# The constant of every fourth unit, added by GpSimd instead of shifted in by TensorE

## The chip, the core and the metric

The kernel runs on one core of one Trainium2 chip. The metric is the device time of one execution in microseconds. The engines are named as the profile names them: PE (TensorE, with PEld for its weight loads), DVE (VectorE), ACT (ScalarE), GpSimd (POOL in the rows) and SP, which only starts transfers here.

## The reference

An attention over 32 inducing points, twice (first the points attend to the rows of x, then each row of x to the 32 results), and then, on its output, a layer with a rational activation:

```python
h = mab(I, x)                  # 32 inducing points attend to 12480 rows, 4 batches
x = mab(x, h)                  # each of the 49920 rows attends to the 32 results
h = x @ w_in                   # 128 -> 2048
P = a[0] + a[1] * h + a[2] * h**2 + a[3] * h**3
Q = 1.0 + np.abs(b[0]) * np.abs(h) + np.abs(b[1]) * h**2
out = (P / (Q + 1e-06)) @ w_out    # 2048 -> 128
```

## The kernel before

**Units.** A block is 480 rows of x; there are 26 of them in each of 4 batches. The 2048 columns of h are worked in 8 *units* of 2 x 128 columns, q = 0 to 7 of a block: 832 units in all, each a tile of 128 x 960. Two neighbouring units, 2k and 2k + 1, are a *pair* and share one tile u of 128 x 1920.

**What a unit goes through.** `first` makes h (scaled) on PE, two f16 matmuls into a PSUM tile hp; there are 3 such tiles. From h comes the magnitude, u = |h|. Then l = (u + k1) * (h + k2) is made, on DVE. On ACT, u becomes a logarithm and then a sigmoid, over whole pairs in place. Behind that, l = (l + k3) * u is made. `second` multiplies l by w_out on PE into the PSUM tile po, two f32 matmuls (four rows of the trace) in a unit.

**Even and odd units.** Where k2 enters h differs:

- An odd unit's h comes with k2 from its weights, and ACT takes the magnitude with k2 taken off again (the rows ACTIVATE u<-hp,all).
- An even unit's h comes without k2. DVE takes the magnitude by masking the sign bit (TENSOR_SCALAR u<-hp), and after that `moved` adds k2 to h in PSUM by two f16 matmuls of constants, 96 x 128 by 96 x 480: the *shift* (rows MATMUL hp<-same,by with LDWEIGHTS by). The DVE product l<-u,all,hp of that unit comes after the shift.

**Ticks.** `fast_ticks` writes the order of everything by hand; the instructions keep it on every engine. Tick t starts unit t:

- PE: the second half of unit t - 15, `first` of unit t + 1 between its two matmuls, and at an even t the shift of unit t.
- DVE: at an even t the mask of unit t; at an odd t the product l<-l,all,u of unit t - 13, which is even; at every t the product l<-u,all,hp of unit t - 1.
- GpSimd: at an odd t the product of the odd unit t - 12, `last_on_pool`, in two instructions: an add u<-l,all into the u of unit t - 13 and a product l<-u. The add writes where DVE's product of the same tick reads, and so waits for it.
- ACT: the magnitude at an odd t, and one logarithm or sigmoid of a pair in every tick, four and four in turn, with a table load at each change.

`side` then gives out the work of the attention and of the next batch (the tiles pd, a, asm, hl, pc, e and others) in portions, by a budget for DVE, GpSimd and PE that grows with each tick. `fetch` copies a finished po to oT on DVE, once in a block, in the tick of unit 7, before the product of unit t - 13. A GpSimd instruction of `side` stands in the same queue as the others. `general_ticks` is for other values of a and b and is not run here.

All operations go through one recording helper, so every row of the profile has its line, 177; the rows are told apart by their tiles.

Of the kernel before, what the change touches and what calls it, by code (L numbers as in the profile page):

```python
# [16 lines left out]
ALU = mybir.AluOpType  # L17
# [175 lines left out]
class Kernel:  # L193
# [350 lines left out]
    def plain(self, t):  # L544
        return t if self.fast else t.bitcast(F32)
# [343 lines left out]
    def fast_ticks(self, units):  # L889

        V, A, p = self.nc.vector, self.nc.scalar, self.params
        n = len(units)
        at = lambda t: units[t] if 0 <= t < n else None
        plain = lambda u: not self.shifted(u.key[2])

        def mask(u):
            V.tensor_scalar(out=u.u.bitcast(I32), in0=u.h.bitcast(I32), scalar1=0x7FFFFFFF, scalar2=None, op0=ALU.bitwise_and)  # L900

        self.first(units[0])
        for t in range(n + BEHIND + 3):
            u, last, d, done = at(t), at(t - 1), at(t - BEHIND), at(t - BEHIND - 2)
            group, turn = divmod(t - TURNS - 2, 2 * TURNS)
            w = at(2 * TURNS * group + 2 * (turn % TURNS))
            late = done and done.key[2] == 0
            if done and not late:
                self.second(done, (0,))
            if at(t + 1):  # L910
                self.first(at(t + 1))
            if done and not late:
                self.second(done, (1,))
            if u:
                if t % 2 == 0:
                    u.pair = self.mp.tile([P, 2, 2, BT], F32, tag="u", name=f"u{u.i}", bufs=self.rooms["u"])
                    u.u = u.pair[:, 0]
                    mask(u)
                else:
                    u.u = last.pair[:, 1]  # L920
                    if not plain(u):
                        A.activation(u.u, u.h, AF.Abs, bias=p.z_back, scale=1.0)
            if late:
                self.fetched = self.fetch()
            if t % 2 and d:
                V.scalar_tensor_tensor(out=d.g, in0=d.g, scalar=p.z_k3, in1=d.u, op0=ALU.add, op1=ALU.mult)
                self.last_on_pool(at(t - BEHIND + 1), d)
            if u and t % 2 and plain(u):
                mask(u)
            if last:  # L930
                last.g = self.new(last, "l")
                V.scalar_tensor_tensor(out=last.g, in0=last.u, scalar=p.z_k1, in1=last.h, op0=ALU.add, op1=ALU.mult)
            if u and plain(u):
                self.moved(u)
            self.run_act(turn == TURNS)
            if w and turn < TURNS:
                A.activation(w.pair, w.pair, AF.Ln, bias=LAM, scale=LAM / Z)
            elif w:
                A.activation(w.pair, w.pair, AF.Sigmoid, bias=p.lnc, scale=-2.0)
            self.side(u or units[-1])  # L940
            if late:
                self.second(done)
        self.fetch()
# [170 lines left out]
```

## Time and profile before

| | |
|---|---|
| median of 3 runs | 2430.82 us (2430.80 to 2431.76) |
| the profiled execution's own time | 2437.1 us |
| its span, first to last instruction | 2435.3 us |
| busy in the span: PE | 2241.4 us (92%) |
| ACT | 2235.6 us (92%) |
| DVE | 2160.0 us (89%) |
| GpSimd | 1450.1 us (60%) |
| mean granted clock of TensorE | 0.964 |

The busy time is a union: instructions of one engine overlap a little at their ends. An engine is idle where its next instruction waits; the rows name what ended the wait. The first 150 us are start-up, with the first batch's attention and the conversion of the weights, and hold few units.

### The profile page before, as it was taken

Reading aid. Unit: us, or ns where it says so; the run is one execution under the profiler, and the core shown is the slowest. Engines: PE = TensorE matmul, PEld = TensorE weight load, DVE = VectorE, ACT = ScalarE, POOL = GpSimd, SP = SyncE. Lnnn points to the kernel's source line nnn. Section 1 sums busy time; section 2 is a strip of 40 time slices with the busy share of each in tenths; the row PEclk is TensorE's granted clock in tenths of the full one; section 3 lists DMA queues with packets and bytes.
Section 4 is the critical chain, followed back from the end, with each engine's and each line's share of the span. In section 5 each row is a group of like instructions: output and inputs, shape, how many; then the busy total and the mean of one; then the engine's idle time right before and its main releaser. Section 6 shows DMA issues by size and latency. Waiting matters only on the chain.

```text
span 2435.3 us, 25780 instructions
## 1 busy us (share of the span) xinstructions
PE 2241.4 (92%) x8462; PEld 1079.8 (44%) x8462; DVE 2160.0 (89%) x2386; ACT 2235.6 (92%) x1590; POOL 1450.1 (60%) x997
## 2 busy tenths in 40 slices
PE   4379999899999999999999899999999999999997
PEld 2244544344545444444445444444444444444443
DVE  1679999889999988999999889989999999999995
ACT  1069999999989999999899999999999999999996
POOL 0315666566656666666566666756666666666666
PEclk7569999999999999999999999999999999999999
DMA  9312210032022211310222130001101000000000
GB/s 236 85 33 85 81 50 17 13 85 65 25 65 82 77 42 42 79 50 29 85 82 59 31 90 29 17 13 53 49 21 41 29 17 28 17 18 20 13 16 18
DMA packets 117113, 121.03 MB, mean 50 GB/s; under 512 B 13289, under 2 KB 115561, under 8 KB 116969
## 3 DMA queue, kind: packets, MB, share of 16 engines
q1 hardware_dynamic: 116969, 119.28, 17.5%
q8 instruction: 69, 1.13, 0.2%
q14 instruction: 75, 0.61, 0.1%
HBM read 80.89 MB, written 25.56 MB: 44 GB/s over the span
## 4 chain that ended last, share of the span: by engine, by line
PE 37%; ACT 31%; DVE 16%; issue 10%; SPq 2%; DMA 2%; POOL 1%; DVEq 0%; POOLq 0%; ACTq 0%
ACT u L177 25%; PE po L177 22%; PE hp L177 9%; DVE l L177 8%; ACT L177 5%; DVE u L177 3%; PE pd L177 3%; SPq L177 2%; DMA xTw<-x_c 1%; DVE cv L177 1%; DVE asm L177 1%; PE pgt L177 1%; PE pl L177 1%; DMA at<-hl 1%; POOL l L177 1%
## 5 line engine op out<-in xcount | busy, mean ns | idle before, releaser
L177 PE MATMUL po<-l,w_out 128*128 128x480 f32 x3328 | 1572.9, 577 | 6.5 <-POOL l L177 4.9
L177 DVE SCALAR_TENSOR_TENSOR l<-u,all,hp 128x960 f32<-128x960 f32 x832 | 1003.8, 1207 | 110.6 <-ACT u L177 95.8
L177 POOL TENSOR_TENSOR l<-u 128x960 f32<-128x960 f32 x416 | 930.9, 2238 | 34.6
L177 POOL TENSOR_SCALAR u<-l,all 128x960 f32<-128x960 f32 x416 | 445.4, 1071 | 824.1 <-DVE l L177 714.6
L177 PEld LDWEIGHTS po<-l,w_out 128*128 128x128 f32 x3328 | 619.0, 192 | 385.8 <-issue 220.0
L177 ACT ACTIVATE u<-u,all 128x1920 f32<-128x1920 f32 x416 | 775.4, 1888 | 1.2
L177 ACT ACTIVATE u<-u 128x1920 f32<-128x1920 f32 x416 | 738.0, 1798 | 9.9 <-DVE l L177 8.7
L177 PE MATMUL hp<-at,st 128*128 128x480 f16 x1664 | 480.8, 371 | 60.1 <-DVE l L177 52.7
L177 DVE SCALAR_TENSOR_TENSOR l<-l,all,u 128x960 f32<-128x960 f32 x416 | 529.5, 1273 | 4.8 <-ACT u L177 4.8
L177 DVE TENSOR_SCALAR u<-hp 128x960 int32<-128x960 int32 x416 | 477.2, 1147 | 27.8 <-PE hp L177 26.1
L177 ACT ACTIVATE u<-hp,all 128x960 f32<-128x960 f32 x416 | 435.1, 1046 | 50.5 <-PE hp L177 46.4
L177 PEld LDWEIGHTS <-st 128*128 128x128 f16 (+1 forms) x1872 | 182.5, 98 | 554.6 <-issue 538.5
L177 ACT ACT_TABLE_LOAD x234 | 300.2, 1283 | 4.7 <-PEq L1107 0.7
L177 PE MATMUL hp<-same,by 96*128 96x480 f16 x832 | 239.3, 368 | 48.1 <-DVE u L177 41.7
L177 PEld LDWEIGHTS <-by 96*128 96x128 f16 x832 | 82.0, 99 | 239.1 <-issue 211.7
L177 DVE COPY oT<-po 128x480 f32<-128x480 f32 x104 | 67.9, 653 | 52.8 <-PE po L177 52.5
L177 PEld LDWEIGHTS pd<-HT,xTb 128*120 128x120 f32 x832 | 101.6, 195 | 15.8 <-issue 12.2
L177 PE MATMUL pd<-HT,xTb 128*120 128x32 f32 x832 | 97.9, 273 | 1.5 <-DMA xTb<-x_c 1.5
L177 PE MATMUL po<-at,st 128*128 128x480 f16 x208 | 59.1, 366 | 0.0
L177 ACT ACTIVATE a<-a 120x512 f32<-120x512 f32 (+2 forms) x21 | 14.9, 727 | 42.0 <-DVE a L177 41.9
L177 ACT ACTIVATE e<-e,nmc 128x960 f32<-128x960 f32 (+1 forms) x16 | 15.6, 993 | 32.9 <-DVE nmc L177 32.8
L177 PE MATMUL pa<-ident,a 120*128 120x120 f32 (+1 forms) x112 | 17.4, 281 | 28.8 <-DVE a L177 25.0
(110 smaller groups left out, 610.4 us busy)
## 6 DMA issues: line engine op xcount, KB each, us to landing
xTb<-x_c SPq DMA_DIRECT2D x104, 240.0 KB, 2.8
out<-oT SPq DMA_DIRECT2D x104, 240.0 KB, 2.0
xTa<-x_c SPq DMA_DIRECT2D x78, 240.0 KB, 3.5
x<-x_t SPq DMA_DIRECT2D x78, 240.0 KB, 4.5
at<-hl SPq DMA_DIRECT2D x416, 30.0 KB, 1.8
xw<-x_t SPq DMA_DIRECT2D x8, 720.0 KB, 14.2
xTw<-x_c SPq DMA_DIRECT2D x5, 960.0 KB, 12.6
raw<-w_in SPq DMA_DIRECT2D x4, 480.0 KB, 11.2
```

Of the source, the lines that this page charges most:

```text
L177: ins = call(*args, **kw)
```

## The change

In units 2 and 6 of a block (q % 4 == 2, every other even unit) the shift on PE is left out, so that their h stays without k2. Right after the mask of unit t, in tick t, GpSimd makes u + k1 into a new tile l, one instruction of 128 x 960. In tick t + 1 DVE's product of the unit is (h + k2) * l, where it was (u + k1) * h. Units 0 and 4 keep the shift, the odd units are as before.

```diff
-        V, A, p = self.nc.vector, self.nc.scalar, self.params
+        V, A, G, p = self.nc.vector, self.nc.scalar, self.nc.gpsimd, self.params
         n = len(units)
         at = lambda t: units[t] if 0 <= t < n else None
         plain = lambda u: not self.shifted(u.key[2])
+        added = lambda u: u.key[2] % 4 == 2
@@
             if u and t % 2 and plain(u):
                 mask(u)
-            if last:
+            if last and added(last):
+                V.scalar_tensor_tensor(out=last.g, in0=last.h, scalar=p.z_k2, in1=last.g, op0=ALU.add, op1=ALU.mult)
+            elif last:
                 last.g = self.new(last, "l")
                 V.scalar_tensor_tensor(out=last.g, in0=last.u, scalar=p.z_k1, in1=last.h, op0=ALU.add, op1=ALU.mult)
-            if u and plain(u):
+            if u and added(u):
+                u.g = self.new(u, "l")
+                G.tensor_scalar(out=u.g, in0=u.u, scalar1=1.0, scalar2=p.z_k1, op0=ALU.mult, op1=ALU.add)
+            elif u and plain(u):
                 self.moved(u)
```

GpSimd's queue, in the first batch. The names are tile, block, q and a running number, so l_7_6 is the l of block 7, unit 6. First before, then with the change:

```order
L177 TENSOR_SCALAR u_6_0_1552<-l_6_1_1580,all 128x960
L177 TENSOR_TENSOR l_6_1_1580<-u_6_0_1552 128x960
L177 TENSOR_SCALAR u_6_2_1578<-l_6_3_1629,all 128x960
L177 TENSOR_TENSOR l_6_3_1629<-u_6_2_1578 128x960
L177 TENSOR_SCALAR u_6_4_1627<-l_6_5_1670,all 128x960
```

```order
L177 TENSOR_SCALAR u_6_0_1540<-l_6_1_1568,all 128x960
L177 TENSOR_TENSOR l_6_1_1568<-u_6_0_1540 128x960
L177 TENSOR_SCALAR l_7_6_1790<-u_7_6_1786,all 128x960
L177 TENSOR_SCALAR u_6_2_1566<-l_6_3_1616,all 128x960
L177 TENSOR_TENSOR l_6_3_1616<-u_6_2_1566 128x960
```

The new add of unit 6 of block 7 stands behind the add and product for units 0 and 1 of block 6, and ahead of those for units 2 and 3.

DVE's queue around the same unit, before and with the change:

```order
L177 TENSOR_SCALAR u_7_6_1801<-hp_7_6_1772 128x960
L177 SCALAR_TENSOR_TENSOR l_7_5_1803<-u_7_4_1763,all,hp_7_5_1759 128x960
L177 COPY oT_5_1808<-po_5_0_1689 128x480
L177 SCALAR_TENSOR_TENSOR l_6_2_1610<-l_6_2_1610,all,u_6_2_1578 128x960
L177 SCALAR_TENSOR_TENSOR l_7_6_1827<-u_7_6_1801,all,hp_7_6_1772 128x960
```

```order
L177 TENSOR_SCALAR u_7_6_1786<-hp_7_6_1757 128x960
L177 SCALAR_TENSOR_TENSOR l_7_5_1788<-u_7_4_1748,all,hp_7_5_1744 128x960
L177 COPY oT_5_1793<-po_5_0_1675 128x480
L177 SCALAR_TENSOR_TENSOR l_6_2_1570<-l_6_2_1570,all,u_6_2_1566 128x960
L177 SCALAR_TENSOR_TENSOR l_7_6_1790<-hp_7_6_1757,all,l_7_6_1790 128x960
```

The order stays; the last of the five reads the tile l that GpSimd writes in place of u.

PE's queue behind the matmuls of po at that place, before and with the change:

```order
L177 LDWEIGHTS by
L177 MATMUL hp_7_6_1772<-same,by 128x480
L177 LDWEIGHTS by
L177 MATMUL hp_7_6_1772<-same,by 128x480
L177 LDWEIGHTS st_618
L177 MATMUL hp_8_0_1820<-at_2_0_1515,st_618 128x480
```

```order
L177 LDWEIGHTS st_618
L177 MATMUL po_5_0_1675<-at_1_0_1104,st_618 128x480
L177 LDWEIGHTS st_618
L177 MATMUL hp_8_0_1805<-at_2_0_1504,st_618 128x480
```

The two shift matmuls and their weight loads are gone, and the first product of the next unit follows at once.

## Rows read from the trace of the kernel before

**Rows 1.** The page: each engine's busy time in us, its share of the span, and its instructions.

```profile
span 2435.3 us, 25780 instructions
PE 2241.4 (92%) x8462; PEld 1079.8 (44%) x8462; DVE 2160.0 (89%) x2386; ACT 2235.6 (92%) x1590; POOL 1450.1 (60%) x997
```

**Rows 2.** The table of stages: the stretch, its length, and each engine's busy time in it.

```profile
150.00:700.00 550.00, 520.23 (x2048) 258.92 (x2048) 497.88 (x530) 524.98 (x373) 329.16 (x230) 0.96 0.19 55
700.00:1200.00 500.00, 480.27 (x1906) 233.81 (x1908) 465.30 (x502) 481.90 (x344) 310.44 (x218) 0.99 0.20 57
1200.00:1700.00 500.00, 481.30 (x1870) 231.09 (x1863) 464.59 (x495) 489.06 (x349) 317.77 (x220) 1.00 0.18 50
1700.00:2100.00 400.00, 382.65 (x1298) 182.92 (x1297) 376.19 (x356) 398.81 (x279) 255.40 (x158) 0.99 0.09 29
2100.00:2400.00 300.00, 282.54 (x851) 124.37 (x850) 273.58 (x253) 299.16 (x206) 192.69 (x118) 1.00 0.05 18
sum 2250.00, PE 2146.99 PEld 1031.10 DVE 2077.54 ACT 2193.90 POOL 1405.45; mean PE 429.40 PEld 206.22 DVE 415.51 ACT 438.78 POOL 281.09
```

The columns behind the length are PE, PEld, DVE, ACT and POOL busy, then the granted clock of TensorE, the share of the DMA engines and GB/s.

**Rows 3.** The list of waits between 150 and 2400 us: who waited for whom, us in total, times, the longest.

```profile
DVE l L177 <- ACT u L177: 95.8, 97, 3.4
PE hp L177 <- DVE l L177: 51.2, 84, 4.6
DVE oT L177 <- PE po L177: 40.1, 35, 2.4
PE hp L177 <- DVE u L177: 39.1, 34, 2.7
ACT u L177 <- PE hp L177: 35.3, 32, 4.8
DVE u L177 <- PE hp L177: 18.1, 19, 3.5
DVE l L177 <- PE hp L177: 11.8, 14, 2.9
ACT u L177 <- DVE l L177: 8.7, 14, 3.0
```

**Rows 4.** DVE in order of time, two pairs of units late in the run: start, duration in us, and in brackets the idle time before and what ended it. The mask at 2340.48 is that of a unit 2, the product l<-u,all,hp at 2343.93 the same unit's.

```profile
2338.23 1.21 DVE L177 SCALAR_TENSOR_TENSOR l<-l,all,u 128x960 f32<-128x960 f32 x1
2339.36 1.21 DVE L177 SCALAR_TENSOR_TENSOR l<-u,all,hp 128x960 f32<-128x960 f32 x1
2340.48 1.15 DVE L177 TENSOR_SCALAR u<-hp 128x960 int32<-128x960 int32 x1
2341.55 1.21 DVE L177 SCALAR_TENSOR_TENSOR l<-u,all,hp 128x960 f32<-128x960 f32 x1
2342.67 1.34 DVE L177 SCALAR_TENSOR_TENSOR l<-l,all,u 128x960 f32<-128x960 f32 x1
2343.93 1.20 DVE L177 SCALAR_TENSOR_TENSOR l<-u,all,hp 128x960 f32<-128x960 f32 x1
2345.06 1.15 DVE L177 TENSOR_SCALAR u<-hp 128x960 int32<-128x960 int32 x1
2347.28 1.21 DVE L177 SCALAR_TENSOR_TENSOR l<-u,all,hp 128x960 f32<-128x960 f32 x1 [1.08 <-ACT u L177]
```

**Rows 5.** GpSimd in order of time in the same stretch.

```profile
2339.61 1.07 POOL L177 TENSOR_SCALAR u<-l,all 128x960 f32<-128x960 f32 x1 [1.92 <-DVE l L177]
2340.76 2.23 POOL L177 TENSOR_TENSOR l<-u 128x960 f32<-128x960 f32 x1
```

**Rows 6.** ACT in order of time in the same stretch: the magnitude of one odd unit.

```profile
2346.20 1.04 ACT L177 ACTIVATE u<-hp,all 128x960 f32<-128x960 f32 x1
```

**Rows 7.** The page's groups of instructions: count, busy us, mean ns of one, and the idle time before them with what ended most of it.

```profile
L177 DVE SCALAR_TENSOR_TENSOR l<-u,all,hp 128x960 f32<-128x960 f32 x832 | 1003.8, 1207 | 110.6 <-ACT u L177 95.8
L177 POOL TENSOR_SCALAR u<-l,all 128x960 f32<-128x960 f32 x416 | 445.4, 1071 | 824.1 <-DVE l L177 714.6
L177 DVE SCALAR_TENSOR_TENSOR l<-l,all,u 128x960 f32<-128x960 f32 x416 | 529.5, 1273 | 4.8 <-ACT u L177 4.8
L177 PE MATMUL hp<-same,by 96*128 96x480 f16 x832 | 239.3, 368 | 48.1 <-DVE u L177 41.7
```

**Rows 8.** GpSimd and DVE in order of time at two places where the two meet, around 1224 and around 2401 us.

```profile
1224.08 1.05 POOL L177 TENSOR_TENSOR a<-a,asm 120x512 f32<-120x512 f32 x1
1224.36 1.78 DVE L177 SCALAR_TENSOR_TENSOR l<-l,all,u 128x960 f32<-128x960 f32 x1
...
2401.00 1.21 DVE L177 SCALAR_TENSOR_TENSOR l<-l,all,u 128x960 f32<-128x960 f32 x1
2401.26 1.89 POOL L177 TENSOR_SCALAR u<-l,all 128x960 f32<-128x960 f32 x1 [1.92 <-DVE l L177]
```

**Rows 9.** DVE in order of time: the two products that bound the first, and the two that bound the last, of the 205 intervals with a changed unit between 150 and 2400 us; in the last, the copy between them.

```profile
158.74 1.22 DVE L177 SCALAR_TENSOR_TENSOR l<-l,all,u 128x960 f32<-128x960 f32 x1
168.12 1.21 DVE L177 SCALAR_TENSOR_TENSOR l<-l,all,u 128x960 f32<-128x960 f32 x1
...
2389.51 1.21 DVE L177 SCALAR_TENSOR_TENSOR l<-l,all,u 128x960 f32<-128x960 f32 x1
2394.02 0.65 DVE L177 COPY oT<-po 128x480 f32<-128x480 f32 x1
2394.59 1.21 DVE L177 SCALAR_TENSOR_TENSOR l<-l,all,u 128x960 f32<-128x960 f32 x1
```

**Rows 10.** PE in order of time in the stretch of rows 4: the first product of the odd unit whose magnitude stands in rows 6.

```profile
2340.62 0.57 PE L177 MATMUL hp<-at,st 128*128 128x480 f16 x2
```

## The prediction

> **What bounds the kernel now.** The page is read first. Its engine shares name no single bound: PE 92%, ACT 92% and DVE 89% of a span of 2435.3 us [rows 1]. A start-up stage of some 150 us with little of the main loop blurs them, so the table of stages is read next [rows 2]. Between 150 and 2400 us, 2250 us in all, ACT is busy for 2193.9, PE for 2147.0, DVE for 2077.5 and GpSimd for 1405.5 us. ACT is the bound: it stands at 99.7% from 1700 us on, and is 25.0, 18.1 and 10.9 us short of the three stages before. In those stages PE is close behind it (520 of 550, 480 and 481 of 500 us).
>
> The list of waits tells why ACT falls short [rows 3]. ACT waits 35.3 us for a first product, 8.7 for DVE. PE waits 51.2 us for DVE to leave a PSUM buffer, and 39.1 us with the shift in hand, for the magnitude that has to be taken first. DVE waits 95.8 us for ACT and 40.1 + 18.1 + 11.8 = 70.0 us for PE; all its idle time in the five stages is 2250 - 2077.5 = 172.5 us. So two engines (ACT, PE) are tight, DVE has 7.7% to spare, GpSimd 38%.
>
> Last the order in time, for two pairs of units late in the run [rows 4 to 6]. I call the DVE product of a stored l and a stored u the *late product* (the rows l<-l,all,u); one stands in each pair. Look at what GpSimd does behind it: the late product ends at 2339.44, GpSimd's add starts at 2339.61, its product ends at 2340.76 + 2.23 = 2342.99. DVE comes to the next late product at 2342.67, and that one takes 1.34 us instead of 1.21: it ends 1.02 us after GpSimd's product.
>
> **What the change takes away.** 416 of the 832 shift matmuls, with their weight loads. They are 239.3 us of PE's time [rows 7], so 119.7 us go, 0.575 us in each changed unit. In the five stages 205 changed units lie, whose 118 us take PE from 2147 to 2029 us. Half of PE's 39.1 us of waiting for the magnitude goes too.
>
> **What it adds.** In each of the 208 changed units GpSimd makes one add of 128x960. The trace has this form: 1071 ns [rows 7]. 208 x 1.071 = 223 us bring GpSimd to 1673 us, 69% of the span: throughput is no question. DVE's instructions stay the same in number; the product of a changed unit reads one PSUM and one SBUF operand as before (1207 ns), with their places exchanged. I price that at nothing; no row has the exchanged form, the nearest are 1207 ns and, with both operands in SBUF, 1.21 us [rows 4], so both ends lie together. ACT's list does not change.
>
> **Where the add stands.** GpSimd's queue holds it behind the add and product of the tick before, and DVE's late product of the next tick meets it. From [rows 4, 5]: 0.17 us after a late product's end GpSimd begins 1.07 us of add, 0.08 later 2.23 us of product: done at +3.55. The new add can start at about +3.6 and ends at +4.68. DVE, without other work, is at its next late product at 2342.67 - 2339.44 = +3.2.
>
> These two operations do not run at once. [rows 8] show it both ways. GpSimd's 120x512 product runs from 1224.08 to 1225.13; a late product begun at 1224.36 ends at 1226.14, 1.01 later, and took 1.78 us. And a GpSimd add begun at 2401.26, while a late product ran to 2402.21, took 1.89 us: done 0.94 us after it. So there are two cases. If GpSimd's add is first, the late product ends at 4.68 + 1.01 = 5.7 us after the one before. If the late product is first (it waits already while GpSimd's product runs), it ends at 4.57 as now, but the add is done only at about 5.5, and the product of the changed unit, the next in DVE's queue, waits for that instead: from 4.49 to 5.56. Both cost about 1.1 us against the shortest interval of 4.57 (2339.44 to 2344.01). Behind the waiting DVE instruction stand the next magnitude and the next unit's product, and PE waits for the PSUM buffer that these leave.
>
> The Trainium skill's page "SBUF — State Buffer" (SBUF: two separate sides) says that DVE with two SBUF inputs and GpSimd take a shared port pair for a whole instruction, and that the loser starts about 115 ns after the winner's end. The rows agree that one blocks the other; but 1.01 us is 0.2 less than the 1.21 of an undisturbed late product, where that sentence makes it 1.21 + 0.115. By the page the interval would be an estimated 6.0 us and the time, all else alike, an estimated 48 us longer (0.31 for each of the 154 intervals below); the measured 1.01 is what the sum takes.
>
> **The price in all.** For each changed unit between 150 and 2400 us I take the interval from the end of a late product to the end of the next, in which its add falls, and price it at what is missing to 5.70. The first is 159.96 to 169.33, 9.37 us, price 0; the last 2390.72 to 2395.80, 5.08 us, price 0.62 (the oT copy of 0.65 fills part of it, as in every unit 6) [rows 9]. Of 205 intervals 154 are shorter than 5.70. By stage the prices sum to 22.2, 23.8, 25.4, 27.9 and 24.9 us, 124 us in all.
>
> **What of it shows.** Where DVE waits for ACT afterwards, it costs nothing. In [rows 4] the price is 1.1 us, and three instructions on DVE stands idle for 1.08 us until ACT's magnitude of 2346.20 is done [rows 6]: it would come just in time. So the price is set against DVE's idle time of each stage, its length less its busy time in [rows 2]:
>
> - 150 to 700: 52.1 us idle, price 22.2. DVE rises to 520, beside ACT 525; PE falls to 493.
> - 700 to 1200: 34.7, price 23.8. DVE 489 passes ACT's 482; PE 455.
> - 1200 to 1700: 35.4, price 25.4. DVE 490, ACT 489; PE 455.
> - 1700 to 2100: 23.8, price 27.9. DVE would need 404 us of 400.
> - 2100 to 2400: 26.4, price 24.9. DVE 298.5, ACT 299.2.
>
> DVE ends at 2077.5 + 124 = 2202 us beside ACT's 2194. PE leaves the front, DVE takes its place, and where ACT and PE were two tight engines now ACT and DVE are. What two such engines lose to each other is read from now: 25, 18 and 11 us over the busiest in the first three stages. After, I take: first stage 525 + 22 = 547 (-3, as the third engine has fallen away); second 489 + 14 = 503 (+3); third 490 + 14 = 504 (+4); fourth 404 + 3 = 407 (+7); last 299.2 + 1.5 = 301 (+1). The sum is +12 us. The overheads of 14 and 3 are chosen between nothing (489, 490 and 404 alone would give -11, -10 and +4) and the whole of today's.
>
> The profiled execution took 2437.1 us, 1.8 over its span, and 6.3 above the median of 2430.82. 2437.1 + 12 = 2449 for such an execution, 2443 for the median.
>
> **The rivals.**
> *PE was what held ACT up* (faster). ACT's 35.3 us of waiting for a first product and DVE's 70.0 us of waiting for PE are both for an engine that loses 118 us, and DVE's lateness stays within ACT's slack. For it: a first product that ends at 2340.62 + 0.57 = 2341.19 [rows 10] is read by ACT only at 2346.20 [rows 6], 5.0 us later. Against it: PE itself waits most for DVE, 51.2 us, and DVE gets later. With about 60% of ACT's 35.3 us won, 21 us: 2410.
> *It hides* (no change). ACT sets the pace at 97.5% and every price meets a DVE wait for ACT, as in [rows 4]; 95.8 us of such waits stand against 124 less what falls in the loose first stage. 2431.
> *The price does not find the idle time* (clearly slower). DVE's 172.5 us of idle time stand in other pairs than the prices, so that half of the 124 us comes through: +62, 2493. It decides where DVE's lateness from several pairs in a row exceeds what a first product lies ready before ACT takes it. Its edge is a late product that starts afresh behind the add: 0.2 us more in 154 intervals, 31 us more of price.
>
> **Chances.** The forecast 0.46 (its own range 2434 to 2462), PE relief 0.24, hidden 0.17, clearly slower 0.13. A measurement of this kernel can tell about 0.2%, 5 us, from no change; so faster 0.24, same 0.18 (the hidden case and the forecast's lower edge), slower 0.58. The range takes most of the relief case and the slow case's lower part: 2408 to 2474.
>
> **What the changed profile would show.** Shift matmuls 416 at the same mean; GpSimd's adds 624. If the exclusion is right, the late product's mean rises from 1273 to about 1400 ns and some GpSimd adds take near 2 us; DVE waits for GpSimd appear, at most 69 x 1.1 = 76 us (69 of the intervals are shorter than 4.7). DVE's waits for ACT should shrink from 95.8 to under 60. DVE should stand above 97% from 1700 us on, PE at 90%. The forecast is wrong if ACT's wait for first products falls by over 20 us with DVE's waits for ACT unchanged (relief), or if the late product's mean stays below 1300 (no meeting). It is wrong upwards if ACT falls below 97% after 1700 us.

## The result and the profile after

The change makes the kernel slower: 2465.78 us median of 4 runs (2464.32 to 2471.79) against 2431.29 us, a ratio of 1.0138 with a 95% interval of 1.0123 to 1.0153. That is 34 us, where the forecast was 12; the time lies above the forecast's own range of 2434 to 2462. The profiled execution has a span of 2465.1 us, 29.8 more than before [rows 1].

The page of the changed kernel, each engine's busy time:

```profile
span 2465.1 us, 24742 instructions
PE 2179.7 (88%) x8046; PEld 1032.2 (42%) x8046; DVE 2205.8 (89%) x2386; ACT 2240.1 (91%) x1590; POOL 1741.3 (71%) x1205
```

PE lost 61.7 us, not 120. DVE has the same number of instructions and 45.8 us more of busy time. GpSimd has the 208 new adds.

The page's groups that answer to [rows 7]:

```profile
L177 DVE SCALAR_TENSOR_TENSOR l<-l,all,u 128x960 f32<-128x960 f32 x416 | 575.2, 1383 | 4.8 <-ACT u L177 4.8
L177 DVE SCALAR_TENSOR_TENSOR l<-hp,all,l 128x960 f32<-128x960 f32 x208 | 251.8, 1211 | 81.8 <-POOL l L177 81.8
L177 POOL TENSOR_SCALAR l<-u,all 128x960 f32<-128x960 f32 x208 | 295.7, 1422 | 30.9 <-DVE u L177 29.5
L177 PE MATMUL hp<-same,by 96*128 96x480 f16 x416 | 121.1, 372 | 45.4 <-DVE u L177 39.3
```

The late product went from 1273 to 1383 ns. The product of a changed unit takes 1211 ns by itself, and DVE stood idle 81.8 us ahead of it, waiting for GpSimd's add. The add takes 1422 ns on average where the form takes 1071: it is held up too. PE still waits 39.3 us for magnitudes with half as many shifts.

From DVE's list of waits over the whole span, the rows of the units and of the copy, first of before and then with the change:

```profile
DVE l L177 <- ACT u L177: 100.6, 98, 4.8
DVE oT L177 <- PE po L177: 52.5, 37, 11.1
DVE u L177 <- PE hp L177: 26.1, 22, 3.5
DVE l L177 <- PE hp L177: 13.8, 16, 2.9
```

```profile
DVE l L177 <- POOL l L177: 81.8, 83, 2.2
DVE oT L177 <- PE po L177: 47.3, 28, 12.2
DVE l L177 <- ACT u L177: 23.9, 28, 4.8
DVE u L177 <- PE hp L177: 18.5, 17, 3.5
DVE l L177 <- PE hp L177: 7.6, 9, 1.5
```

This gives the account of the 29.8 us on DVE. Busy time rose by 45.8 (the late products, 416 x 0.110) and waits for GpSimd by 81.8: a price of 127.6 us. Waits for ACT gave back 100.6 - 23.9 = 76.7, the three waits for PE 92.4 - 73.4 = 19.0, smaller ones 2.1. 127.6 - 97.8 = 29.8. This is bookkeeping: it says where DVE's time went, not what set the pace. On ACT the same 29.8 us are 4.5 of busy time, 15.6 more of waiting for first products, 8.7 more of waiting for DVE's products, and 1.0 of other waits. Its two lists, before and with the change:

```profile
ACT u L177 <- PE hp L177: 46.4, 34, 9.0
ACT u L177 <- DVE l L177: 8.7, 14, 3.0
```

```profile
ACT u L177 <- PE hp L177: 62.0, 47, 5.9
ACT u L177 <- DVE l L177: 17.4, 30, 2.9
```

The change was profiled a second time (the change again, below): span 2451.8 us, the same price of 128.9, 78.0 back from ACT's waits, 28.6 from those for PE. Of the 13.3 us between the two profiles 7.2 lie in the start-up, ahead of the first stage. A few us of such an account are therefore chance.

A changed unit late in the run. DVE, then GpSimd, then PE in order of time:

```profile
2208.13 1.20 DVE L177 SCALAR_TENSOR_TENSOR l<-u,all,hp 128x960 f32<-128x960 f32 x1
2209.25 1.34 DVE L177 SCALAR_TENSOR_TENSOR l<-l,all,u 128x960 f32<-128x960 f32 x1
2211.58 1.22 DVE L177 SCALAR_TENSOR_TENSOR l<-hp,all,l 128x960 f32<-128x960 f32 x1 [0.98 <-POOL l L177]
...
2219.91 1.81 DVE L177 SCALAR_TENSOR_TENSOR l<-l,all,u 128x960 f32<-128x960 f32 x1
2221.64 1.20 DVE L177 SCALAR_TENSOR_TENSOR l<-hp,all,l 128x960 f32<-128x960 f32 x1
```

```profile
2207.34 2.24 POOL L177 TENSOR_TENSOR l<-u 128x960 f32<-128x960 f32 x1
2209.55 1.99 POOL L177 TENSOR_SCALAR l<-u,all 128x960 f32<-128x960 f32 x1
...
2219.65 1.07 POOL L177 TENSOR_SCALAR l<-u,all 128x960 f32<-128x960 f32 x1
```

```profile
2209.79 1.77 PE L177 MATMUL po<-l,w_out 128*128 128x480 f32 x4
2212.85 0.56 PE L177 MATMUL hp<-at,st 128*128 128x480 f16 x2 [1.29 <-DVE l L177]
```

Both cases of the prediction stand here. At 2209.25 the late product is first: it ends at 2210.59, the add, issued at 2209.55, is done at 2211.54, and DVE idles 0.98 us ahead of the changed unit's product. That product leaves its PSUM tile at 2212.80, and PE, which stood ready, starts the next first product at 2212.85 after 1.29 us of waiting. At 2219.91 the add (a unit 6, behind the copy) is first: it ends at 2220.72, the late product at 2221.72, 1.00 later. DVE does not wait behind it; PE waits 0.17 us for the PSUM tile of that unit's product.

### The profile page after: what moved, and what is told of

It reads as the page before. It is cut to its first block, busy times and chain, and to the rows that moved or that the text cites. A ratio compares the mean times of both kernels' runs of the same rounds, so it can differ in the third digit from the quotient of the medians.

```text
span 2465.1 us, 24742 instructions
## 1 busy us (share of the span) xinstructions
PE 2179.7 (88%) x8046; PEld 1032.2 (42%) x8046; DVE 2205.8 (89%) x2386; ACT 2240.1 (91%) x1590; POOL 1741.3 (71%) x1205
## 4 chain that ended last, share of the span: by engine, by line
DVE 39%; PE 21%; ACT 14%; issue 12%; POOL 10%; SPq 2%; DMA 2%; DVEq 0%; POOLq 0%; ACTq 0%
DVE l L177 23%; PE po L177 12%; ACT u L177 11%; DVE u L177 8%; POOL l L177 7%; PE hp L177 4%; PE pd L177 3%; POOL u L177 2%; ACT L177 2%; SPq L177 2%; DVE oT L177 2%; DVE asm L177 2%; DMA xTw<-x_c 1%; DVE cv L177 1%; DVE e L177 1%
## 5 line engine op out<-in xcount | busy, mean ns | idle before, releaser
L177 DVE SCALAR_TENSOR_TENSOR l<-u,all,hp 128x960 f32<-128x960 f32 x624 | 750.8, 1203 | 27.4 <-ACT u L177 19.1
L177 PE MATMUL hp<-at,st 128*128 128x480 f16 x1664 | 481.3, 371 | 145.2 <-DVE l L177 139.5
L177 DVE SCALAR_TENSOR_TENSOR l<-l,all,u 128x960 f32<-128x960 f32 x416 | 575.2, 1383 | 4.8 <-ACT u L177 4.8
L177 PEld LDWEIGHTS <-st 128*128 128x128 f16 (+1 forms) x1872 | 175.2, 98 | 663.1 <-issue 488.1
L177 DVE SCALAR_TENSOR_TENSOR l<-hp,all,l 128x960 f32<-128x960 f32 x208 | 251.8, 1211 | 81.8 <-POOL l L177 81.8
L177 POOL TENSOR_SCALAR l<-u,all 128x960 f32<-128x960 f32 x208 | 295.7, 1422 | 30.9 <-DVE u L177 29.5
L177 PE MATMUL hp<-same,by 96*128 96x480 f16 x416 | 121.1, 372 | 45.4 <-DVE u L177 39.3
L177 PEld LDWEIGHTS <-by 96*128 96x128 f16 x416 | 40.9, 98 | 161.2 <-issue 154.6
```

The lines of the kernel that those rows point to most:

```text
L177: ins = call(*args, **kw)
```

## The experiments

Three questions were open: is the price what the prediction says (the exclusion of GpSimd and the late product); what is PE's relief worth; and why does more come through than forecast. Medians are compared with those of before in the same rounds, as ratios.

**PE's relief alone.** The shift of units 2 and 6 is left out, nothing is put in its place.

```diff
-            if u and plain(u):
+            if u and plain(u) and u.key[2] % 4 != 2:
                 self.moved(u)
```

> The kernel before, with the shift of units 2 and 6 left out and nothing in its place (their h lacks k2, so that part of the computation is missing). It shows what 120 us less on PE are worth alone. Theory A (GpSimd's add stops DVE, and PE's relief is worth something): 2410 to 2420 us; ACT's wait for first products falls from 46 us to about 25. Theory B (PE's relief is worth nothing, ACT and DVE set the time): 2431 within 5 us. Theory C (PE was what held the kernel up): below 2405 us.

Measured: 0.9970 (0.9957 to 0.9982), 7 us. Its page, and its shifts among the groups:

```profile
PE 2181.1 (90%) x8046; PEld 1033.6 (43%) x8046; DVE 2159.2 (89%) x2386; ACT 2234.9 (92%) x1590; POOL 1448.6 (60%) x997
L177 PE MATMUL hp<-same,by 96*128 96x480 f16 x416 | 121.2, 373 | 42.9 <-DVE u L177 36.5
```

The shift's group lost 118 us, PE only 60: 0.29 us in each changed unit instead of 0.575. A matmul's row overlaps that of its neighbour, as in the kernel before, where the two shift matmuls have 0.57 us and the next row starts 0.41 us after them:

```profile
2341.82 0.57 PE L177 MATMUL hp<-same,by 96*128 96x480 f16 x2
2342.23 0.97 PE L177 MATMUL po<-l,w_out 128*128 128x480 f32 x2
```

So the relief is half of what was counted and is worth 7 us: less than theory A's 11 to 21, a little more than theory B allows, and C is out. ACT's wait for first products fell from 46.4 to 38.6 us, where theory A had 25.

**The add without the relief.** The shift stays on PE, the add and the product come as with the change.

```diff
-                V.scalar_tensor_tensor(out=last.g, in0=last.h, scalar=p.z_k2, in1=last.g, op0=ALU.add, op1=ALU.mult)
+                V.scalar_tensor_tensor(out=last.g, in0=last.h, scalar=0.0, in1=last.g, op0=ALU.add, op1=ALU.mult)
...
-            elif u and plain(u):
+            if u and plain(u):
                 self.moved(u)
```

> The change, with the shift of units 2 and 6 kept on PE; DVE's product adds 0 instead of k2, so the result is the reference's. GpSimd's add comes without PE's relief. Theory A: slower than the change by what the relief is worth, 2476 to 2495 us; DVE's waits for GpSimd near 80 us and a late product of 1380 ns, as with the change. Theory B: 2466 within 5 us, as the time is DVE's alone.

Measured: 1.0105 (1.0086 to 1.0123), no slower than the change. So it was run again with the change itself in the same rounds.

> The change itself, on the chip and in the rounds of the next kernel, so that the two can be set side by side. All theories: 1.012 to 1.015 times the kernel before.

> The change with the shift of units 2 and 6 kept (DVE adds 0, the result is the reference's), beside the change on one chip: the earlier run of it came out at 1.0105, below the change's 1.0138 of another day. Theory F (once the add stands in GpSimd's queue, PE waits for DVE, and relief on PE buys nothing): the same as the change within 3 us. Theory A (relief is worth 10 us or more whatever else stands): slower than the change by 7 us or more.

Measured: the change 1.0115 (1.0094 to 1.0137), with the shift kept 1.0119 (1.0101 to 1.0137). The change's first measurement was a little higher; here it stays below what was expected of it. The two kernels do not differ. That does not show that the relief is worth nothing beside the add, because the two differ in one more thing: the product that adds the number 0 reads no column `all` and is shorter.

```profile
L177 DVE SCALAR_TENSOR_TENSOR l<-hp,l 128x960 f32<-128x960 f32 x208 | 239.5, 1151 | 82.8 <-POOL l L177 81.4
```

With 1151 ns in place of 1211 it gives DVE 12 us back, and DVE's busy time and its waits for the add come to 114 us more than before, 13 less than with the change. By the table of the other units below, 13 us there are worth an estimated 3 to 8 us of time (0.25 to 0.64 for each, between neighbouring rows), about as much as the relief of 7. What the rounds show is that the add slows the kernel by 1% with the shift kept as without it. PE's waits for DVE's products in the change (139.5 us), and in the kernel with neither shift nor add (91.4, in the page's group of first products):

```profile
PE hp L177 <- DVE l L177: 139.5, 208, 4.2
```

```profile
L177 PE MATMUL hp<-at,st 128*128 128x480 f16 x1664 | 483.4, 373 | 99.0 <-DVE l L177 91.4
```

It was 52.7 us before. So 39 of the 87 us come without any add, as PE, with less to do, is earlier at the PSUM tile; the other 48 come with the add, as DVE leaves the tile later when it has waited for GpSimd.

**The exclusion without the wait.** GpSimd adds into a tile that nobody reads; the shift is left out.

```diff
+            if u and added(u):
+                G.tensor_scalar(out=self.aside, in0=u.u, scalar1=1.0, scalar2=p.z_k1, op0=ALU.mult, op1=ALU.add)
-            if u and plain(u):
+            elif u and plain(u):
                 self.moved(u)
```

> Units 2 and 6 without shift; GpSimd makes its add, into a tile of bf16 that nobody reads, and DVE's product reads u as before (k2 is missing from these units). The add stands in GpSimd's queue as with the change, but no DVE instruction waits for it. Theory A (the exclusion of GpSimd and the late product is the cause; who waits for whom is of no matter): 2450 to 2466 us; the late product's mean goes above 1450 ns, since what waited for the add now meets GpSimd's later product. Theory D (the data dependence is the cause, 82 us of waiting): 2425 to 2440 us, with the late product's mean at or below 1400 ns.

Measured: 1.0011 (1.0001 to 1.0021), 10 us above the kernel without shift. Its late product:

```profile
L177 DVE SCALAR_TENSOR_TENSOR l<-l,all,u 128x960 f32<-128x960 f32 x416 | 589.2, 1417 | 4.8 <-ACT u L177 4.8
```

Theory A's time is out and theory D's is right, but the mean of 1417 lies between theory D's 1400 and theory A's 1450. The late products cost 59.7 us more of their own time, the waiting of 82 us is gone, and little comes through.

**Exclusion by what?** The same kernel with a fill of that tile in the add's place, which reads nothing.

```diff
-                G.tensor_scalar(out=self.aside, in0=u.u, scalar1=1.0, scalar2=p.z_k1, op0=ALU.mult, op1=ALU.add)
+                G.memset(self.aside, 1.0)
```

> As the kernel with the add that nobody reads, but in the add's place GpSimd fills that tile with a constant: 128x960 of bf16, no input from SBUF, by a 96x480 fill of 494 ns about 0.95 us long (k2 is missing from units 2 and 6). It stands at the same place of GpSimd's queue. If GpSimd and the late product exclude each other for their inputs alone: the late product's mean falls back to 1273 ns and the time to that of the kernel without the shift, 0.997 of before. If any GpSimd instruction holds the late product up: a mean of about 1400 ns, as with the unread add, and 1.001 of before.

Measured: 0.9961 (0.9947 to 0.9974), as without the shift.

```profile
L177 DVE SCALAR_TENSOR_TENSOR l<-l,all,u 128x960 f32<-128x960 f32 x416 | 530.2, 1275 | 4.8 <-ACT u L177 4.8
L177 POOL MEMSET aside<- 128x960 bf16 x208 | 187.1, 900 | 0.3
```

The late product is back at 1275 ns with 0.90 us of GpSimd at the same place of the queue. The fill is shorter than the add and does not wait for the mask, so it has to be seen that the two still meet: 150 late products of the trace run beside a fill. Of the 78 with the fill begun first, 67 meet nothing else on GpSimd, and these take 1207 ns on average, such as

```profile
2179.63 0.90 POOL L177 MEMSET aside<- 128x960 bf16 x1
2180.01 1.21 DVE L177 SCALAR_TENSOR_TENSOR l<-l,all,u 128x960 f32<-128x960 f32 x1
```

It is the add's reading that holds the late product up. The Trainium skill's page "SBUF — State Buffer" (SBUF: two separate sides) says the same: two SBUF inputs on DVE conflict only with a GpSimd operation that reads SBUF.

**Other units.** Units 4 and 6 in place of 2 and 6, then 6 alone, then all even units.

```diff
-        added = lambda u: u.key[2] % 4 == 2
+        added = lambda u: u.key[2] in (4, 6)      # then == 6, then % 2 == 0
```

> The change with units 4 and 6 in place of 2 and 6: the same number of shifts, adds and products. DVE's other work in the interval of a unit 4 is 0.78 us on average, in that of a unit 2 it is 0.34 us, and the add can run beside it. Theory A: 0.44 x 102 = 45 us less of price on DVE, of which a third to a half shows: 2443 to 2452 us. Theory E (what counts is GpSimd's 223 us more of work, or PE's instructions): 2466 within 5 us.

> The change in unit 6 alone: 104 adds, 208 shift matmuls fewer. The price in the intervals of unit 6 sums to 32 us, and DVE waits for ACT some 30 us in the intervals right behind, those of unit 0. Theory G (DVE's price comes through where no DVE wait for ACT follows it, and is absorbed where one does): 2428 to 2434 us on the basis of 2431 for before, the same within 0.2%. Theory H (a fixed third of the price comes through, beside half of the relief's 7 us): plus 7 us, 2438.

> The change in all even units, 0, 2, 4 and 6: 416 adds, no shift on PE at all. Every interval between late products then has an add in it. Theory A's floor (no such interval can be below 5.70 us): 409 intervals of at least 5.70, longer where DVE's own work is, sum to 2367 us, with 204 us outside them 2570 us. Theory H (a fixed third of the price of 209 us): about 2495 us.

Measured: units 4 and 6 at 1.0063 (1.0042 to 1.0084), 15 us on the basis of 2431, inside theory A's band. Unit 6 alone at 0.9998 (0.9988 to 1.0008), theory G's "the same". All even units at 1.0477 (1.0456 to 1.0499), 2553 us by the median of two runs, 0.7% under the floor's 2570 and far from theory H's 2495. The nearness to 2570 is partly luck: 260 of that kernel's 415 intervals between late products are shorter than 5.70 us, as the wait for the add falls behind a late product that came first, and others are longer. From DVE's waits with all even units:

```profile
DVE l L177 <- POOL l L177: 190.8, 193, 4.9
DVE oT L177 <- PE po L177: 46.5, 23, 11.1
DVE l L177 <- ACT u L177: 4.3, 5, 1.7
```

The waits for ACT are used up, those ahead of the copy are as they were. Laid side by side, with the price as DVE's busy time over the 2160.0 us of before plus its wait for the add, both from each kernel's page and list of waits:

| kernel | price, us | DVE's waits for ACT | ratio |
|---|---|---|---|
| before | 0 | 100.6 | 1 |
| fill, not an add | 2 | 99.0 | 0.9961 |
| unit 6 | 29.4 + 6.9 = 36 | 75.1 | 0.9998 |
| add that nobody reads | 54.4 + 0 = 54 | 68.3 | 1.0011 |
| units 4 and 6 | 37.7 + 37.8 = 76 | 60.4 | 1.0063 |
| the change with the shift kept | 33.0 + 81.4 = 114 | 26.6 | 1.0105, 1.0119 |
| the change | 45.8 + 81.8 = 128 | 23.9 | 1.0138, 1.0115 |
| all even units | 69.2 + 190.8 = 260 | 4.3 | 1.0477 |

In these kernels the time rises with the price, slowly while DVE still waits for ACT, and steeply when those waits are gone: from the change to all even units the price rises by 132 us and the time by 82 to 88 us of 2431. The rows differ in their shifts too, which is worth up to 7 us for 208 of them.

**The copy of the finished block.** If DVE's wait ahead of oT were only an order that is badly chosen, the copy could be moved behind the products of its tick. It was moved in the change and in the kernel before.

```diff
-            if late:
-                self.fetched = self.fetch()
             if t % 2 and d:
...
+            if late:
+                self.fetched = self.fetch()
             if u and added(u):
```

> The change, with the copy of the finished block (oT from po) put in DVE's queue behind the two products of its tick instead of ahead of them. With the change DVE stands idle 45 to 47 us ahead of this copy, for PE to finish the block, although PE has 118 us less to do. Theory F (PE is late there because it waits for DVE's products, which then wait behind the copy: a ring): 10 to 25 us faster than the change, 2440 to 2455, with the idle time ahead of the copy below 20 us. Theory I (the copy is late because PE has its work to do; moved, the wait comes back elsewhere, PE now waiting for the copy): the same as the change within 4 us.

> The kernel before with the same move of the copy and nothing else, so that the move's own worth is known. ACT is at 97.5% and DVE has slack: theory F expects 2425 to 2432 us (the same), theory I the same or up to 5 us slower.

Measured: 1.0115 (1.0094 to 1.0137) and 0.9997 (0.9986 to 1.0007): no change in either, and the wait ahead of the copy stays (51.3 and 50.6 us). Theory F's ring through the copy falls.

**The product behind the next mask.** The add gets 1.1 us more to arrive.

```diff
+            if held and t % 2 == 0:
+                V.scalar_tensor_tensor(out=held.g, in0=held.h, scalar=p.z_k2, in1=held.g, op0=ALU.add, op1=ALU.mult)
+                held = None
...
             if last and added(last):
-                V.scalar_tensor_tensor(out=last.g, in0=last.h, scalar=p.z_k2, in1=last.g, op0=ALU.add, op1=ALU.mult)
+                held = last
```

> The change, with DVE's product of a changed unit behind the next mask instead of ahead of it, so that the add has 1.1 us more to arrive; the result is the reference's. Theory D (what comes through is mainly DVE's 82 us of waiting for the add; the late product's stretch meets slack): the wait falls below 15 us and the time to 2432 to 2443 us, as with the add that nobody reads. Theory A (the exclusion costs the same whoever waits): 2455 or more, the late product's mean rising above 1450 ns.

Measured: 1.0210 (1.0189 to 1.0231), the slowest but one. The wait for the add fell to 0.6 us, as theory D says, and the time went the other way; it lies in theory A's band, but the late product's mean of 1363 ns is not above theory A's 1450. From the lists of waits of PE, ACT and DVE:

```profile
PE hp L177 <- DVE l L177: 225.6, 222, 8.0
ACT u L177 <- PE hp L177: 101.7, 73, 5.5
DVE oT L177 <- PE po L177: 70.2, 68, 12.2
DVE u L177 <- PE hp L177: 57.1, 68, 4.4
```

A changed unit's product now leaves its PSUM tile one mask later in DVE's order, PE waits 225.6 us for such tiles (139.5 with the change), and DVE and ACT then wait for PE. ACT's wait rose by 40 us over that of the change while DVE's price fell to 37. So there is a second way for a delay on DVE to cost time, beside DVE's own total: through the three PSUM tiles to PE.

## Why the prediction was wrong in size

**The bound and the sign: right.** ACT was the bound and DVE took PE's place behind it. From 1700 to 2100 us of the changed kernel DVE is busy for 371.3 us and waits 18.4 us for the add, 389.7 of 400 together, the 97% that was named, if the waits count (busy alone is 93%). ACT is busy for 388.8 of these 400 us, 97.2%: the sign of being wrong upwards, below 97%, did not show, although the time went up.

**The price: right.** 1.1 us for each meeting and 124 us in the five stages were forecast; 45.8 + 81.8 = 127.6 us were measured over the span. The late product was put at about 1400 ns, it has 1383; waits for GpSimd at 69 of 1.1 us, 76 at most, there are 83 of 0.99, a little more; waits for ACT at under 60, there are 23.9. The exclusion, the two cases and the 1.0 us behind a meeting stand in the rows above, and the run with the fill shows that the add's reading is what does it.

**The relief: mis-sized by half.** The step "They are 239.3 us of PE's time [rows 7], so 119.7 us go, 0.575 us in each changed unit." took matmul rows as time on PE. PE's busy time fell by 60 us in the run that only leaves the shift out; a row overlaps the next. The 0.57 us of [rows 10] could not warn, as it is the same sum of rows; the 0.41 us to the next row, shown with the run without the shift, could: 208 x 0.41 = 85 us, nearer, though still above 60. In the first three stages PE therefore did not fall as far as forecast (505.6, 463.3 and 461.1 us, not 493, 455 and 455), and the rival that rested on it, to which 0.24 was given, had 7 us to win, not 21.

**What of it shows: the step that failed.** "So the price is set against DVE's idle time of each stage" took all of that idle time, 172.5 us, as time that can give way: 95.8 us of waits for ACT and 70.0 of waits for PE. The first gave way as thought (76.7 us over the span). The second did so in small part: over the span 19.0 of 92.4 us, 28.6 in the second profile. The missing shift alone takes 12.1 from them and the add with the shift kept 8.2. From 1700 to 2100 us, where ACT was at 99.7%, waits for PE are all that DVE has left beside its work and the add:

```profile
DVE l L177 <- POOL l L177: 18.4, 19, 1.0
DVE oT L177 <- PE po L177: 6.6, 3, 2.7
DVE u L177 <- PE hp L177: 3.5, 3, 1.8
```

In the sum this is the term of the overheads, "chosen between nothing" and "the whole of today's". From the mask of the same pair to the mask of the same pair, the third and fourth stage of the changed kernel, in the columns of [rows 2]:

```profile
1205.10:1716.20 511.10, 469.43 (x1771) 221.29 (x1764) 473.38 (x495) 490.52 (x349) 381.04 (x267) 0.99 0.18 49
1716.20:2130.00 413.80, 371.66 (x1222) 174.30 (x1222) 383.82 (x356) 402.18 (x280) 313.67 (x196) 0.99 0.09 28
```

DVE with its 18.3 and 18.4 us of waits for the add comes to 491.7 and 402.2 us, ACT to 490.5 and 402.2, where 490 and 404 were forecast for DVE and 489 and 399 stand for ACT in [rows 2]. So the work and the price in these stages were sized rightly. Over the larger of the two the stages lost 19.4 and 11.6 us, where 14 and 3 had been chosen; in the fourth, 11.3 of the 11.6 are DVE's waits for PE. The five stages ran 3.1, 6.0, 12.8 and 13.4 us longer and 2.5 shorter, 32.8 together, where -3, +3, +4, +7 and +1 were forecast (in the second profile -2.3, +5.5, +10.7, +15.7 and -2.5, 27.1 together). The term of 12 us should have been about 30.

**The rivals.** That the change hides is what happens at a quarter of the price: unit 6 alone measures 0.9998. Clearly slower, 2493, went too far for this change, but its reason, idle time that the price does not find, is the one that was at work. In the prediction's own words it "decides where DVE's lateness from several pairs in a row exceeds what a first product lies ready before ACT takes it"; ACT's wait for first products rose from 46.4 us over the span to 62.0 (50.1 in the second profile), so a part of it came that way.

**What stays open.** How the 30 us split between DVE's own total and the PSUM tiles is not settled: the table orders the kernels by price, and the product behind the next mask, with a price of 37 us and a ratio of 1.0210, shows that the tiles alone can cost as much, but no run holds one fixed and varies the other. What the relief is worth beside the add is not settled either, nor why PE's busy time fell by 60 us and not by 85. Nor do the runs explain why the waits ahead of the copy stay near 50 us wherever it stands.

No kernel that keeps k2 in all units beat the kernel before. The whole relief is 7 us, and the cheapest place for the add, unit 6, costs as much time as its part of it gives.

## What to carry to other kernels

Price a piece of work moved to a slack engine by what it stands next to, not by that engine's share: GpSimd was at 60%, and 223 us of adds cost DVE 128 us. When a price is set against an engine's idle time, look at what each wait is for: here 77 of 101 us of waits for the bound gave way, but only 19 to 29 of 92 us of waits for PE, which itself waits for DVE's tiles. And take the relief on PE from the spacing of its rows rather than from their durations. A variant that is meant to isolate one cause has to be compared instruction by instruction: a constant in place of a column made one product 60 ns shorter here, which may hide the relief.

## What the runs showed of the hardware

A DVE operation with two SBUF inputs and a GpSimd operation that reads SBUF do not run together. In the change's trace 91 late products started after a new add had begun. In 86 of them the product ended 1.00 us (median) after the add, 0.2 less than the 1.21 that such a product takes alone; in the other 5 it had started only 0.02 to 0.11 us after the add, and the add was held up in its place. The 75 new adds that started behind a late product ended 0.94 us after it, 0.13 less than their 1.07. A late product that already waited behind a GpSimd product came before the GpSimd operation next in the queue in all 79 places where the two stood so. A GpSimd fill of 0.90 us, which reads nothing, leaves the late product at 1207 ns.
